# Values for three head pairs in five loads, keys and queries split and turned sooner, second-layer weight blocks loaded later: attention with a maxout layer on one core

## The chip, the cores and the metric

The kernel runs on one core of one Trainium2 chip. The metric is the device time of one launch in microseconds, as the median of a few runs. The core has TensorE (PE in the profile; its weight loads are PEld), VectorE (DVE), ScalarE (ACT), GpSimd (POOL) and SyncE (SP), which run side by side and wait for each other by semaphores. Transfers are issued by an engine's instruction queue, here nearly all by SP, and carried out by 16 DMA engines.

## The reference

```python
# q, k, v: (8, 12, 448, 64) float32; w1, w2, w3, w_out: (768, 768) float64; x is (3584, 768)
q_n, k_n = (rmsnorm(q, g_q), rmsnorm(k, g_k))
scores = scale * np.matmul(q_n, k_n.transpose(0, 1, 3, 2))
scores = scores - np.max(scores, axis=-1, keepdims=True)
attn = np.exp(scores)
attn = attn / (np.sum(attn, axis=-1, keepdims=True) + 1e-09)
attn_out = np.matmul(attn, v)
x = attn_out.transpose(0, 2, 1, 3).reshape(B * S, H * D)
h = np.maximum(np.maximum(x @ w1, x @ w2), x @ w3)
out = h @ w_out
```

Eight batches of 12 heads go through normalised attention; the heads of a batch side by side are the 448 rows of x that go through the maxout layer.

## The kernel before

**Work and pairs.** Two heads make a pair; there are 48 pairs (`g` = 0 to 47), six to a batch. A pair's 448 x 448 scores are made in four chunks `c` (three of 128 queries for each head, the last of 64 for both). The first six pairs (`PLAIN`) use float32 matmuls and let TensorE turn keys, queries and weights. From pair 6 on, each float32 operand is split into an upper and a lower float16 part, and the turning is done by transposing transfers: `turn_rows` (keys and queries), `turn_weights` (softmax weights, tiles `pp` to `pt`).

**Beats.** `beat(g, i)` writes out the program in order, 12 beats to a pair. No scheduler moves anything afterwards: what is written first on an engine or on a queue goes first there. `later(n, work)` puts work n beats on. Between its score matmuls TensorE gets matmuls of the maxout layer (`thirds`, from `ffn`); that filling exists from pair 6 on, when the first batch's x is done.

**Keys and queries of a pair** (from pair 6 on). `scale_rows` (GpSimd) makes `kn` and `qn` in beats 8 and 9 two pairs ahead. `upper_rows` (ScalarE) casts to float16, `lower_rows` (GpSimd) subtracts, `turn_rows` issues a transposing transfer on SP, and `swap_keys` issues two copies `kt<-kt` on SP that bring each head's keys to the other half of the partitions. Before, these stand in beats 0 and 1, 2 and 3, 4 and 5, and 7 of the pair before. The first scores of a pair are written in beat 11; their second matmul reads what the two copies bring.

**Values.** `load_v(g)` loads one pair's values in four transfers into a tile `vr` (7 buffers). Each row of 64 values is 256 bytes; rows 0 to 63 of one head and 384 to 447 of the other fill the last quarter. Three beats later `largest_v` (VectorE) takes the largest absolute value per row; `bound_v(b)` joins those of a batch and spreads the bound by a matmul (`most<-v_most`). In pair 0 the values of pairs 0 to 6 are loaded in beats 0 to 6, later one pair's in beat 6. `scale_v`, `upper_v` and `lower_v` split the values from pair 6 on; `add_values` multiplies them with `pt` (`av`).

**Weight blocks.** 24 blocks of float64 weights pass through two buffers `raw` of 768 KB: 18 of the first layer, one each 4 beats, then 6 of the second, one each 8 beats. `prep_block(n)` scales a block's upper words (ScalarE, L186), three steps on VectorE over the next beats put float32 together (L194, L198, L203), and 5 beats after it `load_raw` issues the load of block n+2 into the buffer that is then free. The instruction waits in SP's queue for the last VectorE step.

Of the kernel before, what the change touches and what calls it, by code (L numbers as in the profile page):

```python
# [9 lines left out]
F32 = mybir.dt.float32  # L10
# [6 lines left out]
P = 128  # L17
# [18 lines left out]
PLAIN = 6  # L36
# [6 lines left out]
def qknorm_attention_maxout_ffn_kernel(  # L43
# [35 lines left out]
    nc = tc.nc  # L79
    B, H, S, D = q.shape  # L80
    DM, DF = w1.shape
    DO = w_out.shape[1]
    NP = H // 2
    NQ = 4
    UNITS = 7
# [6 lines left out]
    G = B * NP  # L92
# [4 lines left out]
    sb = ctx.enter_context(tc.tile_pool(name="sb", bufs=2))  # L97
# [18 lines left out]
    def later(beats, work, last=False):  # L116

        due.setdefault(clock[0] + beats, ([], []))[last].append(work)
# [63 lines left out]
    def rebias(raw):  # L182


        upper = raw.bitcast(F32).rearrange("p (n t) -> p n t", t=2)[:, :, 1]
        nc.scalar.activation(upper, upper, AF.Copy, scale=REBIAS)  # L186
# [42 lines left out]
    def plain(t, n):  # L229
        return t[:, n + 1].rearrange("p a n -> p (a n)").bitcast(F32)  # L230

    def prep_block(n):
        kind, ft, j = blocks[n]
        raw = raws[n]
        f = plain(w_sb, n) if kind == "in" else plain(wo_sb, ft)
        rebias(raw)

        for stage in range(3):
            later(2 + stage, lambda stage=stage: decode(raw, f, stage), True)
        if kind == "out":  # L240
            later(5, lambda: row_largest(o_row[:, ft:ft + 1], f), True)
        later(5, load_raw)
        if j == NJ - 1:
            later(5, lambda: bound_in(ft), True)
        elif kind == "out" and ft == NFT - 1:
            later(6, bound_out)
# [76 lines left out]
    st = {}  # L323
# [20 lines left out]
        load_rows(g, "kr", k, first if g < LOADS else (nc.scalar,))  # L344


    def load_v(g):

        b, pr = divmod(g, NP)
        t = sb.tile([P, 2, 4, D], F32, name="vr", bufs=7)  # L350
        rows = v[b, 2 * pr:2 * pr + 2]
        for h in range(2):
            nc.sync.dma_start(
                out=t[:, h, 0:3], in_=rows[h, 0:3 * P].rearrange("(u p) d -> p u d", p=P)
            )
        for half, part in zip(HALVES, (rows[:, 3 * P:S], rows[:, 0:LEFT])):
            nc.sync.dma_start(out=t[half, :, 3], in_=part.rearrange("h p d -> p h d"))
        st.setdefault(g, {})["vr"] = t


    def squares(g, what):
        s = st[g]
        src = s[what + "r"]
        sq = sb.tile([P, UNITS, D], F32, name="sq", tag="rows", bufs=5)
        if g < 2:
            nc.scalar.activation(sq, src, AF.Square)  # L366
        else:
            nc.gpsimd.tensor_tensor(out=sq, in0=src, in1=src, op=ALU.mult)
        s["sq" + what] = sq
# [21 lines left out]
    def scale_rows(g, what):  # L391
        s = st[g]
        rows, ri = s.pop(what + "r"), s["ri"][:, KQ[what]]
        n = sb.tile([P, UNITS, D], F32, name=what + "n", tag="rows", bufs=5)
        s[what + "n"] = n
        on = nc.gpsimd if g else nc.vector
        on.tensor_tensor(
            out=n, in0=rows,
            in1=ri.rearrange("p (n o) -> p n o", o=1).broadcast_to([P, UNITS, D]),
            op=ALU.mult,  # L400
        )
        if what == "k":
            return
        s.pop("ri")
        if g >= PLAIN:
            nc.gpsimd.tensor_tensor(
                out=n, in0=n,
                in1=gain.rearrange("p (o d) -> p o d", o=1).broadcast_to([P, UNITS, D]),
                op=ALU.mult,
            )  # L410


    def upper_rows(g, what):
        s = st[g]
        n = s.pop(what + "n")
        parts = sb.tile([P, UNITS, 2, D], F16, name=what + "p", bufs=1)
        nc.scalar.copy(parts[:, :, 0], n)  # L417
        s[what + "p"] = parts, n

    def lower_rows(g, what):  # L420
        s = st[g]
        parts, n = s[what + "p"]
        nc.gpsimd.tensor_tensor(  # L423
            out=parts[:, :, 1], in0=n, in1=parts[:, :, 0], op=ALU.subtract
        )
        s[what + "p"] = parts

    def turn_rows(g, what):
        s = st[g]
        parts = s.pop(what + "p")  # L430
        if what == "k":
            t = sb.tile([P, 2, UNITS * P], F16, name="kt", bufs=2)
            to = t[:, 0].rearrange("p (n r) -> p n r", n=UNITS)
        else:
            t = sb.tile([P, 8, P], F16, name="qt", bufs=2)
            to = t[:, :UNITS]
        nc.sync.dma_start_transpose(out=to, in_=parts.rearrange("p n a d -> p (n a d)"))
        s[what + "s"] = t
# [44 lines left out]
    v_rows = {}  # L483
    v_down = const.tile([P, B], F32, name="v_down")
    v_up = const.tile([P, B], F32, name="v_up")

    def largest_v(g):
        b, pr = divmod(g, NP)
        if b not in v_rows:
            v_rows[b] = sb.tile([P, NP], F32, name="v_rows", bufs=2)  # L490
        row_largest(
            v_rows[b][:, pr:pr + 1], st[g]["vr"].rearrange("p h n d -> p (h n d)")
        )

    def bound_v(b):
# [21 lines left out]


    def scale_v(g):
        vr = st[g]["vr"].rearrange("p h n d -> p (h n d)")  # L520
        nc.gpsimd.tensor_scalar(
            out=vr, in0=vr, scalar1=v_up[:, g // NP:g // NP + 1], scalar2=1.0,
            op0=ALU.mult, op1=ALU.mult,
        )

    def upper_v(g):
        s = st[g]
        vp = sb.tile([P, 2, 8, D], F16, name="vp", bufs=2)
        nc.scalar.copy(vp[:, 0], s["vr"].rearrange("p h n d -> p (h n) d"))  # L529
        s["vp"] = vp  # L530

    def lower_v(g):
        s = st[g]
        vr, vp = s.pop("vr"), s["vp"]
        nc.gpsimd.tensor_tensor(  # L535
            out=vp[:, 1], in0=vr.rearrange("p h n d -> p (h n) d"), in1=vp[:, 0],
            op=ALU.subtract,
        )

# [76 lines left out]
    def pt_plain(s):  # L616
        return s["pt"].rearrange("p u s -> p (u s)").bitcast(F32).rearrange(
            "p (h u s) -> p h u s", h=2, u=4
        )
# [113 lines left out]
    def add_values(g):  # L733
        s = st[g]
        av = ps_a.tile([P, 512], F32, name="av", tag="a")
        s["av"] = av
        if g < PLAIN:
            vr, pt = s["vr"], pt_plain(s)
            for u in range(4):
                rows = HALVES[0] if u == 3 else slice(0, P)  # L740
                for h, half in enumerate(HALVES):
                    nc.tensor.matmul(
                        av[half, :S], vr[rows, h, u], pt[rows, h, u],
                        start=u == 0, stop=u == 3,
                    )
            return
        vp, vs, pt = s["vp"], s["vs"], s["pt"]
        steps = [(part, u, u) for u in range(4) for part in range(2)]
        steps += [(2, u, 4 + u) for u in range(3)]
        for n, (part, u, block) in enumerate(steps):  # L750
            for h, half in enumerate(HALVES):
                values = vs[:, h, u] if part == 2 else vp[:, part, 4 * h + u]
                nc.tensor.matmul(  # L753
                    av[half, :S], values, pt[:, 7 * h + block, SHIFT[h]:SHIFT[h] + S],
                    start=n == 0, stop=n == len(steps) - 1,
                )
# [150 lines left out]
    for i, src in enumerate((g_q, g_k)):  # L907
        nc.scalar.dma_start(
            out=gains[:, i], in_=src.rearrange("(o d) -> o d", o=1).broadcast_to([P, D])
# [75 lines left out]
    def beat(g, i):  # L985
        w, n = g - 1, g + 2
        c, part = divmod(i, 3)
        k = 4 * g + c
# [41 lines left out]
        if g + 1 < G:  # L1030
            if g + 1 < PLAIN:
                if i in (1, 4):
                    turn_whole(g + 1, "kq"[i // 4])
                if i in (2, 5):
                    keep_whole(g + 1, "kq"[i // 5])
            else:
                if i in (0, 1):
                    upper_rows(g + 1, "kq"[i])
                if i in (2, 3):
                    lower_rows(g + 1, "kq"[i - 2])  # L1040
                if i in (4, 5):
                    turn_rows(g + 1, "kq"[i - 4])
                if i == 7:
                    swap_keys(g + 1)

        if n < G:
            if i in (0, 3):
                squares(n, "kq"[i // 3])
            if i in (2, 5):
                sum_squares(n, "kq"[i // 3])  # L1050
            if i in (5, 7):
                inv_rms(n, "kq"[i // 7])
            if i in (8, 9):
                scale_rows(n, "kq"[i - 8])

        if g == 0 and i < 7:
            load_v(i)
            later(3, lambda: largest_v(i))
        if 0 < g < G - 6 and i == 6:
            load_v(g + 6)  # L1060
            later(3, lambda: largest_v(g + 6))
        if g == 0 and i == 9:
            bound_v(0)
        if g > 1 and g % NP == 0 and g < G and i == 1:
# [66 lines left out]
```

## Time and profile before

| what | value |
|---|---|
| median of 3 runs | 1071.95 us (1071.87 to 1072.58) |
| the profiled execution | 1070.58 us, of which span 1068.8 us |
| PE busy | 992.4 us, 93% of the span |
| DVE, ACT, POOL busy | 705.5, 637.9, 615.2 us |
| mean granted TensorE clock | 0.974 |
| transfers of one pair's values | 2 of 96 KB and 2 of 32 KB, 192 in all |

In the views, L753 is line 753 of the kernel, `out<-in` names what an instruction writes and reads, `x12` is a count. A row of the waits reads: engine, output and line that waited, what it waited for, total us, times, longest. A row of the timeline reads: start, duration, engine, line, operation, and in brackets the idle time of the engine before it with what ended it. "SPq" is SP's queue. A row of the windows gives busy time and instruction count of PE, PEld, DVE, ACT and POOL, then the granted clock, the mean busy share of the DMA engines and GB/s.

### The profile page before, as it was taken

What the parts mean: (1) busy time and instruction counts of PE and PEld (TensorE: products, weight loads), DVE (VectorE), ACT (ScalarE), POOL (GpSimd) and SP (SyncE); (2) the same over time, 40 slices, a digit from 0 to 9 for tenths busy, and PEclk for the clock granted to TensorE, in tenths of its full rate; (3) what the DMA queues carried; (4) which work ended last, traced back from release to release, by engine and by line L of the source; (5) the groups of instructions that cost most, each with busy time, mean ns of one, the idle gap of its engine ahead of it and who ended that gap; (6) DMA issues with size and microseconds to landing.
All of it is one profiled execution on the core that took longest, in us unless ns stands there. A gap on an engine that the chain in (4) does not pass through costs nothing. (4 is left out here: it accounts for less than half of the span.)

```text
span 1068.8 us, 17394 instructions
## 1 busy us (share of the span) xinstructions
PE 992.4 (93%) x5850; PEld 527.0 (49%) x5850; DVE 705.5 (66%) x1348; ACT 637.9 (60%) x1437; POOL 615.2 (58%) x661
## 2 busy tenths in 40 slices
PE   5598869899889999999999999999999999999998
PEld 3354434444445555455544555545544555555555
DVE  3789978888757776677666766777577756761110
ACT  3478868657746566565755666657566675652101
POOL 5257878856746767467666675766657666510000
PEclk9699979989989999999999999999999999999999
DMA  5655659896999999999999999999989999672001
GB/s 144 162 146 161 162 154 202 175 178 123 195 180 158 162 177 206 157 183 161 198 164 173 164 189 191 168 169 174 184 169 176 164 194 182 115 121 76 1 1 59
DMA packets 526681, 166.20 MB, mean 156 GB/s; under 512 B 502912, under 2 KB 522368, under 8 KB 526592
## 3 DMA queue, kind: packets, MB, share of 16 engines
q1 hardware_dynamic: 463584, 149.10, 71.7%
q10 hardware_dynamic: 63008, 16.00, 8.3%
q8 instruction: 46, 0.75, 0.3%
q14 instruction: 43, 0.35, 0.1%
HBM read 53.54 MB, written 11.01 MB: 60 GB/s over the span
## 5 line engine op out<-in xcount | busy, mean ns | idle before, releaser
L782 PE MATMUL acc<-xt,w_sb 128*128 128x448 f16 x2592 | 515.4, 354 | 0.0
L782 PEld LDWEIGHTS <-w_sb 128*128 128x128 f16 x2592 | 252.1, 98 | 244.2 <-issue 15.3
L611 ACT ACTIVATE sc<-sc,nm 128x448 f32<-128x448 f32 x294 | 178.8, 608 | 163.7 <-DVE nm L595 159.2
L595 DVE TENSOR_REDUCE nm<-sc 128x2 f32<-128x896 f32 x192 | 186.2, 970 | 95.1 <-PE sc L580 58.2
L697 ACT ACTIVATE pp<-sc,rs 128x448 f16<-128x448 f32 x294 | 172.8, 633 | 119.4 <-issue 65.8
L707 DVE SCALAR_TENSOR_TENSOR pp<-sc,rs,pp 128x448 f16<-128x448 f32 x294 | 187.9, 674 | 3.1 <-ACT pp L697 3.1
L573 PE MATMUL sc<-kt,qt 128*128 128x448 f16 x504 | 121.1, 358 | 34.4 <-DMA kt<-kt 22.5
L389 POOL TENSOR_TENSOR ri<-ri,half_neg 128x7 f32<-128x7 f32 x96 | 147.3, 1535 | 8.0
L842 PE MATMUL acc<-wo_sb,ht 128*128 128x384 f16 x864 | 148.3, 326 | 0.3 <-DVE ht L806 0.3
L811 POOL COPY hx<-ht 128x128 f16<-128x128 f16 x48 | 15.5, 323 | 204.4 <-DVE ht L806 204.4
L842 PEld LDWEIGHTS <-ht 128*128 128x128 f16 x864 | 83.3, 98 | 60.5 <-issue 4.7
L535 POOL TENSOR_TENSOR vp<-vr,vp 128x512 f16<-128x512 f32 x42 | 50.0, 1189 | 76.9 <-ACT vp L529 76.9
L573 PEld LDWEIGHTS <-qt 128*128 128x128 f16 x504 | 47.7, 98 | 86.2 <-DMA kt<-kt 29.1
L423 POOL TENSOR_TENSOR kp<-kn,kp 128x448 f16<-128x448 f32 x42 | 44.9, 1069 | 46.9 <-ACT kp L417 46.8
L753 PE MATMUL av<-pt,vp 128*64 128x448 f16 x672 | 71.6, 356 | 0.0
L375 DVE TENSOR_REDUCE ss<-sq 128x7 f32<-128x448 f32 x96 | 57.8, 603 | 12.5 <-ACT sq L366 9.0
L690 DVE TENSOR_SCALAR rs<-sc 128x2 f32<-128x2 f32 (+1 forms) x168 | 26.2, 156 | 52.7 <-ACT sc L611 52.7
L768 DVE SCALAR_TENSOR_TENSOR xt<-av,xt 128x448 f16<-128x448 f32 x42 | 26.2, 623 | 49.1 <-ACT xt L767 49.1
L423 POOL TENSOR_TENSOR qp<-qn,qp 128x448 f16<-128x448 f32 x42 | 43.4, 1034 | 23.0 <-ACT qp L417 23.0
L168 DVE TENSOR_REDUCE v_rows<-vr 128x1 f32<-128x512 f32 x48 | 32.8, 683 | 33.7 <-DMA vr<-in_v_dram 32.8
L796 DVE TENSOR_TENSOR m<-acc,m 128x448 f32<-128x448 f32 x48 | 29.6, 617 | 36.0 <-PE acc L782 35.3
L753 PEld LDWEIGHTS <-vp 128*64 128x64 f16 x672 | 34.5, 109 | 34.1 <-issue 12.2
(126 smaller groups left out, 1224.4 us busy)
## 6 DMA issues: line engine op xcount, KB each, us to landing
raw<-in_moe_w_dram SPq DMA_DIRECT2D x18, 768.0 KB, 4.5
kt<-kt SPq DMA_DIRECT2D x84, 112.0 KB, 2.3
vr<-in_v_dram SPq DMA_DIRECT2D x96, 96.0 KB, 2.8
out_dram<-osb SPq DMA_DIRECT2D x24, 384.0 KB, 3.5
kr<-in_k_dram ACTq DMA_DIRECT2D x34, 224.0 KB, 3.5
qr<-in_q_dram ACTq DMA_DIRECT2D x34, 224.0 KB, 4.6
raw<-in_moe_w_out_dram SPq DMA_DIRECT2D x6, 768.0 KB, 5.2
vs<-vp SPq DMA_DIRECT2D x84, 48.0 KB, 3.4
```

The source lines that it names most:

```text
L375: nc.vector.tensor_reduce(sums[g % 2][:, KQ[what]], sq, axis=AX, op=ALU.add)
L389: nc.gpsimd.tensor_tensor(out=ri, in0=ri, in1=half_neg[:, at], op=ALU.pow)
L423: nc.gpsimd.tensor_tensor(out=parts[:, :, 1], in0=n, in1=parts[:, :, 0], op=ALU.subtract)
L535: nc.gpsimd.tensor_tensor(out=vp[:, 1], in0=vr.rearrange("p h n d -> p (h n) d"), in1=vp[:, 0], op=ALU.subtract,)
L573: nc.tensor.matmul(sc[:, h, :S], qt[:, 4 * h + c], kt[:, n, keys[h]], start=n == 0, stop=n == 1,)
L595: nc.vector.tensor_reduce(nm[:, :n], sc[:, :n, :S], axis=AX, op=ALU.max, negate=True)
L611: nc.scalar.activation(to, sc[:, h, :S], AF.Exp, bias=nm[:, h:h + 1], accum_out=total,)
L697: nc.scalar.activation(pp[:, h, 0], sc[:, h, :S], AF.Copy, scale=rs[:, h:h + 1])
L707: nc.vector.scalar_tensor_tensor(out=pp[:, h, 1], in0=sc[:, h, :S], scalar=rs[:, h:h + 1], in1=pp[:, h, 0], op0=ALU.mult, op1=ALU.subtract,)
L753: nc.tensor.matmul(av[half, :S], values, pt[:, 7 * h + block, SHIFT[h]:SHIFT[h] + S], start=n == 0, stop=n == len(steps) - 1,)
L782: nc.tensor.matmul(acc[:, :S], wt[:, wp, c], xs[c][:, xp], start=(c == 0 and n == 0), stop=(c == NCT - 1 and n == 2),)
L842: nc.tensor.matmul(acc[:, :HW], lhs, wo_sb[:, f, wp, half * HW:(half + 1) * HW], start=(f == 0 and n == 0), stop=(f == NFT - 1 and n == 2),)
```

## The change

Values are loaded for three pairs at once: a tile holds six heads, in three transfers of 128 partitions x 6 heads x 64 and two of 64 x 6 x 64, with 3 buffers (of three times the size) instead of 7. Tiles 0 and 1 are loaded in beats 0 and 3 of pair 0, tile 2 in its beat 9, and from there one tile in beat 9 of every third pair. The largest value is taken once per tile, 5 or 8 beats after the load. Keys are cast in beat 11 of the pair before the one they were cast in, queries in beat 0 (each one beat sooner); the subtraction, the turning and the copies come two beats sooner (beats 0 and 1, 2 and 3, 5). Blocks loaded from within the second layer's steps are issued 9 beats instead of 5 after the step. The tag `rows` (squares and scaled rows) has 4 buffers instead of 5.

```diff
-        later(5, load_raw)
+        later(5 if kind == "in" else 9, load_raw)
...
-        t = sb.tile([P, 2, 4, D], F32, name="vr", bufs=7)
-        rows = v[b, 2 * pr:2 * pr + 2]
-        for h in range(2):
+        vr = sb.tile([P, NP, 4, D], F32, name="vr", bufs=3)
+        rows = v[b, NP * n:NP * (n + 1)]
+        for u in range(3):
             nc.sync.dma_start(
-                out=t[:, h, 0:3], in_=rows[h, 0:3 * P].rearrange("(u p) d -> p u d", p=P)
+                out=vr[:, :, u],
+                in_=rows[:, u * P:(u + 1) * P].rearrange("h p d -> p h d"),
             )
         for half, part in zip(HALVES, (rows[:, 3 * P:S], rows[:, 0:LEFT])):
-            nc.sync.dma_start(out=t[half, :, 3], in_=part.rearrange("h p d -> p h d"))
+            nc.sync.dma_start(out=vr[half, :, 3], in_=part.rearrange("h p d -> p h d"))
...
+    def values_of(g):
+        return v_tiles[g // 3][:, 2 * (g % 3):2 * (g % 3) + 2]
...
-        sq = sb.tile([P, UNITS, D], F32, name="sq", tag="rows", bufs=5)
+        sq = sb.tile([P, UNITS, D], F32, name="sq", tag="rows", bufs=4)
...
             else:
+                if i == 0:
+                    upper_rows(g + 1, "q")
                 if i in (0, 1):
-                    upper_rows(g + 1, "kq"[i])
+                    lower_rows(g + 1, "kq"[i])
                 if i in (2, 3):
-                    lower_rows(g + 1, "kq"[i - 2])
-                if i in (4, 5):
-                    turn_rows(g + 1, "kq"[i - 4])
-                if i == 7:
+                    turn_rows(g + 1, "kq"[i - 2])
+                if i == 5:
                     swap_keys(g + 1)
 
+        if PLAIN <= n < G and i == 11:
+            upper_rows(n, "k")
...
-        if g == 0 and i < 7:
-            load_v(i)
-            later(3, lambda: largest_v(i))
-        if 0 < g < G - 6 and i == 6:
-            load_v(g + 6)
-            later(3, lambda: largest_v(g + 6))
+        if g == 0 and i in (0, 3):
+            load_v(i // 3)
+            later(5, lambda: largest_v(i // 3))
+        if g % 3 == 0 and g + 6 < G and i == 9:
+            load_v(g // 3 + 2)
+            later(8, lambda: largest_v(g // 3 + 2))
```

On SP's queue in pair 0, before: the values of seven pairs, and then the third and fourth weight block (the number after a name tells buffers apart; line numbers differ between the two programs).

```order
L334 DMA qr_197<-in_q_dram 128x64
L353 DMA vr_215<-in_v_dram 128x3x64 x2
L357 DMA vr_215<-in_v_dram 64x2x64 x2
L333 DMA kr_220<-in_k_dram 128x3x64 x2
L334 DMA kr_220<-in_k_dram 128x64
...
L353 DMA vr_304<-in_v_dram 128x3x64 x2
L357 DMA vr_304<-in_v_dram 64x2x64 x2
L353 DMA vr_330<-in_v_dram 128x3x64 x2
L357 DMA vr_330<-in_v_dram 64x2x64 x2
L221 DMA raw_335<-in_moe_w3_dram 128x6x256
L221 DMA raw_377<-in_moe_w1_dram 128x6x256
```

The same place after:

```order
L334 DMA qr_197<-in_q_dram 128x64
L355 DMA vr_215<-in_v_dram 128x6x64 x3
L360 DMA vr_215<-in_v_dram 64x6x64 x2
L333 DMA kr_221<-in_k_dram 128x3x64 x2
L334 DMA kr_221<-in_k_dram 128x64
L333 DMA qr_232<-in_q_dram 128x3x64 x2
L334 DMA qr_232<-in_q_dram 128x64
L355 DMA vr_263<-in_v_dram 128x6x64 x3
L360 DMA vr_263<-in_v_dram 64x6x64 x2
L221 DMA raw_310<-in_moe_w3_dram 128x6x256
L355 DMA vr_342<-in_v_dram 128x6x64 x3
L360 DMA vr_342<-in_v_dram 64x6x64 x2
```

Ten value loads now stand ahead of the third block where 28 stood, and a third tile's five stand between the third and the fourth.

On SP's queue in a pair in the middle, before, from one pair's key transpose to the copies of its values:

```order
L437 DMA_TRANSPOSE kt<-kp 128x7x128
L437 DMA_TRANSPOSE qt<-qp 128x7x128
L720 DMA_TRANSPOSE pt<-pp 128x14x128
L353 DMA vr<-in_v_dram 128x3x64 x2
L357 DMA vr<-in_v_dram 64x2x64 x2
L444 DMA kt<-kt 64x896 x2
L720 DMA_TRANSPOSE pt<-pp 128x14x128 x2
L726 DMA_TRANSPOSE pt<-pp 128x7x64 x2
L546 DMA vs<-vp 64x2x192
L547 DMA vs<-vp 64x2x192
```

The same after, in a pair with a value load:

```order
L443 DMA_TRANSPOSE kt<-kp 128x7x128
L732 DMA_TRANSPOSE pt<-pp 128x7x64 x2
L443 DMA_TRANSPOSE qt<-qp 128x7x128
L552 DMA vs<-vp 64x2x192
L553 DMA vs<-vp 64x2x192
L450 DMA kt<-kt 64x896 x2
L726 DMA_TRANSPOSE pt<-pp 128x14x128
L824 DMA out_dram<-osb 128x768
L726 DMA_TRANSPOSE pt<-pp 128x14x128
L355 DMA vr<-in_v_dram 128x6x64 x3
L360 DMA vr<-in_v_dram 64x6x64 x2
L726 DMA_TRANSPOSE pt<-pp 128x14x128
```

The key copies stand ahead of the first weight transpose and no value load is in front of them; the key transpose stands ahead of the last chunk's two weight transposes, and the query transpose between these and the copies of the values.

On GpSimd around a pair's end, before:

```order
L521 TENSOR_SCALAR vr<-vr,v_up 128x512
L368 TENSOR_TENSOR sq<-kr 128x448
L535 TENSOR_TENSOR vp<-vr,vp 128x512
L423 TENSOR_TENSOR kp<-kn,kp 128x7x64
L423 TENSOR_TENSOR qp<-qn,qp 128x7x64
L368 TENSOR_TENSOR sq<-qr 128x448
```

And after:

```order
L527 TENSOR_SCALAR vr<-vr,v_up 128x512
L429 TENSOR_TENSOR kp<-kn,kp 128x7x64
L374 TENSOR_TENSOR sq<-kr 128x448
L541 TENSOR_TENSOR vp<-vr,vp 128x512
L429 TENSOR_TENSOR qp<-qn,qp 128x7x64
L374 TENSOR_TENSOR sq<-qr 128x448
```

The lower part of the keys now stands two places up, ahead of the squares and of the values' lower part. TensorE's own order is the same in both programs.

More of the change, by code (lines that the diff above doesn't have):

```diff
@@ L344, in load_k, with load_v @@
         load_rows(g, "kr", k, first if g < LOADS else (nc.scalar,))
-    def load_v(g):
-        b, pr = divmod(g, NP)
-        t = sb.tile([P, 2, 4, D], F32, name="vr", bufs=7)
-        rows = v[b, 2 * pr:2 * pr + 2]
-        for h in range(2):
+    v_tiles = {}
+    def load_v(t):
+        b, n = divmod(t, 2)
+        vr = sb.tile([P, NP, 4, D], F32, name="vr", bufs=3)
+        rows = v[b, NP * n:NP * (n + 1)]
+        for u in range(3):
             nc.sync.dma_start(
-                out=t[:, h, 0:3], in_=rows[h, 0:3 * P].rearrange("(u p) d -> p u d", p=P)
+                out=vr[:, :, u],
+                in_=rows[:, u * P:(u + 1) * P].rearrange("h p d -> p h d"),
             )
         for half, part in zip(HALVES, (rows[:, 3 * P:S], rows[:, 0:LEFT])):
-            nc.sync.dma_start(out=t[half, :, 3], in_=part.rearrange("h p d -> p h d"))
-        st.setdefault(g, {})["vr"] = t
+            nc.sync.dma_start(out=vr[half, :, 3], in_=part.rearrange("h p d -> p h d"))
+        v_tiles[t] = vr
+    def values_of(g):
+        return v_tiles[g // 3][:, 2 * (g % 3):2 * (g % 3) + 2]
     def squares(g, what):
@@ L393, in scale_rows @@
         rows, ri = s.pop(what + "r"), s["ri"][:, KQ[what]]
-        n = sb.tile([P, UNITS, D], F32, name=what + "n", tag="rows", bufs=5)
+        n = sb.tile([P, UNITS, D], F32, name=what + "n", tag="rows", bufs=4)
         s[what + "n"] = n
@@ L485, in qknorm_attention_maxout_ffn_kernel, with largest_v @@
     v_up = const.tile([P, B], F32, name="v_up")
-    def largest_v(g):
-        b, pr = divmod(g, NP)
+    def largest_v(t):
+        b, n = divmod(t, 2)
         if b not in v_rows:
-            v_rows[b] = sb.tile([P, NP], F32, name="v_rows", bufs=2)
+            v_rows[b] = sb.tile([P, 2], F32, name="v_rows", bufs=2)
         row_largest(
-            v_rows[b][:, pr:pr + 1], st[g]["vr"].rearrange("p h n d -> p (h n d)")
+            v_rows[b][:, n:n + 1], v_tiles[t].rearrange("p h n d -> p (h n d)")
         )
@@ L519, in scale_v @@
     def scale_v(g):
-        vr = st[g]["vr"].rearrange("p h n d -> p (h n d)")
+        vr = values_of(g).rearrange("p h n d -> p (h n d)")
         nc.gpsimd.tensor_scalar(
@@ L528, in upper_v @@
         vp = sb.tile([P, 2, 8, D], F16, name="vp", bufs=2)
-        nc.scalar.copy(vp[:, 0], s["vr"].rearrange("p h n d -> p (h n) d"))
+        nc.scalar.copy(vp[:, 0], values_of(g).rearrange("p h n d -> p (h n) d"))
         s["vp"] = vp
@@ L533, in lower_v @@
         s = st[g]
-        vr, vp = s.pop("vr"), s["vp"]
+        vp = s["vp"]
         nc.gpsimd.tensor_tensor(
-            out=vp[:, 1], in0=vr.rearrange("p h n d -> p (h n) d"), in1=vp[:, 0],
+            out=vp[:, 1], in0=values_of(g).rearrange("p h n d -> p (h n) d"), in1=vp[:, 0],
             op=ALU.subtract,
@@ L737, in add_values @@
         if g < PLAIN:
-            vr, pt = s["vr"], pt_plain(s)
+            vr, pt = values_of(g), pt_plain(s)
             for u in range(4):
```

## The prediction

> **What bounds the kernel now.** I read the page first (span, busy shares, slices), then the windows, then TensorE's waits by stage, and last the queue of SP where those waits end.
>
> ```profile
> span 1068.8 us, 17394 instructions
> ...
> PE 992.4 (93%) x5850; PEld 527.0 (49%) x5850; DVE 705.5 (66%) x1348; ACT 637.9 (60%) x1437; POOL 615.2 (58%) x661
> ...
> PE   5598869899889999999999999999999999999998
> ```
>
> ```profile
> 15.00:50.00 35.00, 21.20 (x93) 12.77 (x94) 21.70 (x32) 17.26 (x41) 15.83 (x18) 0.76 0.62 150
> 50.00:135.00 85.00, 76.37 (x457) 43.91 (x458) 76.96 (x100) 68.88 (x144) 60.19 (x46) 0.94 0.56 154
> 135.00:150.00 15.00, 7.89 (x39) 5.16 (x37) 10.02 (x17) 9.28 (x18) 10.50 (x8) 0.77 0.65 178
> 150.00:300.00 150.00, 126.78 (x719) 64.25 (x718) 120.83 (x231) 103.21 (x222) 106.62 (x104) 0.94 0.86 172
> 300.00:900.00 600.00, 590.97 (x3564) 309.13 (x3563) 415.67 (x842) 380.90 (x888) 389.53 (x440) 1.00 0.97 176
> ```
>
> TensorE is the bound from 300 us on: 9 us idle in 600. What can be won lies mostly earlier: 13.8 us idle from 15 to 50, 8.6 from 50 to 135 (there VectorE, 76.96 of 85 us busy, paces the float32 pairs), 7.1 from 135 to 150, 23.2 from 150 to 300. TensorE's order is the same after the change, so the span moves by what its idle time moves. Its waits in all, in 135 to 300, and in 300 to 900:
>
> ```profile
> PE sc L573 <- DMA kt<-kt: 22.5, 13, 6.1
> ...
> PE most L504 <- DVE v_most L497: 8.9, 2, 6.9
> ...
> PE sc L573 <- DMA kt<-kt: 15.0, 4, 6.1
> ...
> PE sc L573 <- DMA kt<-kt: 7.5, 9, 1.8
> ```
>
> The largest waits end on two things that the change touches: the key copies `kt<-kt` (22.5 us), and the bound on the values (one wait of 6.9 us).
>
> **The values at the start.** SP's queue, VectorE's waits from 15 to 50, VectorE's and ScalarE's work there:
>
> ```profile
> 22.65 0.96 SPq L353 DMA_DIRECT2D vr<-in_v_dram  x2
> 23.66 1.25 SPq L357 DMA_DIRECT2D vr<-in_v_dram  x2
> ...
> 37.55 1.26 SPq L357 DMA_DIRECT2D vr<-in_v_dram  x2
> 38.92 3.67 SPq L221 DMA_DIRECT2D raw<-in_moe_w_dram  x2
> ...
> DVE v_rows L168 <- DMA vr<-in_v_dram: 7.3, 6, 2.0
> ...
> 39.54 0.15 DVE L497 TENSOR_REDUCE v_most<-v_rows 128x1 f32<-128x6 f32 x1
> ...
> 51.07 0.55 DVE L194 TENSOR_SCALAR w_sb<-raw 128x768 uint32<-128x768 uint32 x1
> ...
> 43.51 0.88 ACT L186 ACTIVATE raw<-raw 128x768 f32<-128x768 f32 x1 [5.43 <-DMA raw<-in_moe_w_dram]
> ...
> 47.09 0.91 ACT L186 ACTIVATE raw<-raw 128x768 f32<-128x768 f32 x1
> ```
>
> SP issues from 22.65 to 38.81 almost without a break: six pairs' values at 2.2 us each, and one pair's queries. VectorE follows at that pace, `v_most` comes at 39.54, and the third weight block leaves at 38.92, so ScalarE waits 5.4 us for it. The prices:
>
> ```profile
> L353 SPq DMA_DIRECT2D vr<-in_v_dram x96: 367/496/1477, 15.9 to 846.5; - x96
> ...
> L357 SPq DMA_DIRECT2D vr<-in_v_dram x96: 600/630/1190, 17.1 to 847.7; - x96
> ...
> L336 SPq DMA_DIRECT2D kr<-in_k_dram x8: 386/644/1042, 81.9 to 236.8; - x8
> ...
> L168 DVE TENSOR_REDUCE v_rows<-vr x48: 666/686/687, 23.5 to 850.4; 128x1 f32<-128x512 f32 x48
> L168 DVE TENSOR_REDUCE most<-w_sb x6: 2534/2540/2543, 48.6 to 154.5; 128x1 f32<-128x2304 f32 x6
> L168 DVE TENSOR_REDUCE o_row<-wo_sb x6: 933/941/944, 164.5 to 237.2; 128x1 f32<-128x768 f32 x6
> ```
>
> No load of 128x6x64 exists. Its issue is bounded by 0.50 us (128x3x64, L353) below and 1.04 us (the longest of 128x7x64, L336) above; the half-partition ones by 0.63 and 1.19. A tile costs 2.8 to 5.5 us of SP; I take 2.8 at the start, where L353 and L357 run near their medians. Between 22.65 and the third block then stand the queries (16.2 - 6 x 2.2 = 3 us with what lies between) and one tile: SP is free at 28.5 instead of 38.9. The block must also wait for VectorE to be done with the first block. VectorE loses 7.3 us of waits, and two reductions of 1536 elements (941 + 768 x (2540 - 941)/1536 = 1741 ns, 3.5 us) replace six (4.1 us): `v_most` comes some 6.5 to 7.9 us sooner. The fourth block now stands behind a third tile of the same 768 KB; the third alone gains up to 10 us, but the fourth sets VectorE's step at 51.07. I take 6.5 us for the whole start, with ends 0 (the blocks arrive no sooner) and 10.4 (SP's lead in full). It is kept, since VectorE paces what follows and has no other long wait there.
>
> **The first float16 pair.** Here the copies leave 0.5 us behind a weight block:
>
> ```profile
> 137.29 0.38 SPq L221 DMA_DIRECT2D raw<-in_moe_w_dram  x1
> 137.77 1.17 SPq L444 DMA_DIRECT2D kt<-kt  x2
> ...
> 144.58 1.30 PE L573 MATMUL sc<-kt,qt 128*128 128x448 f16 x3 [6.15 <-DMA kt<-kt]
> ...
> 141.55 0.68 DVE L768 SCALAR_TENSOR_TENSOR xt<-av,v_up,xt 128x448 f16<-128x448 f32 x1
> 145.92 1.09 DVE L595 TENSOR_REDUCE nm<-sc 128x2 f32<-128x896 f32 x1 [3.69 <-PE sc L573]
> ...
> DMA to landing us min/median/max: 2.2/2.3/6.5
> ```
>
> They land 6.5 us after issue (the last row, their landings) where 2.3 is usual. Two beats sooner they leave ahead of that block, and the values' four loads (2.2 us) are no longer before them. TensorE's 6.15 us go; VectorE has work until 142.23, so the maximum at 145.92 can come 3.7 us sooner, or 4.4 without the reduction that stood before it. I take 4.0, ends 0 and 6.15. Next late are VectorE's own steps.
>
> **The other key copies.** 15.0 - 6.15 = 8.9 us until 300 and 7.5 later. The copies move two beats (a pair takes 18.9 us, SP's rows below from 340.33 to 359.26; 2 x 18.9/12 = 3.2 us) and lose 2.2 us of value loads in front. With 5.4 us the waits up to 1.8 us after 300 go whole, if their transposes keep up: I take 6.5 of 7.5, ends 3 and 7.5. Of the 8.9 I take 5, since VectorE is busy 120.83 of 150 us there and would be next late; ends 2 and 8.9.
>
> **What the sooner steps push back.** In a pair in the middle:
>
> ```profile
> 340.33 2.56 SPq L726 DMA_TRANSPOSE pt<-pp  x2
> ...
> 349.59 1.71 PE L753 MATMUL av<-pt,vp 128*64 128x448 f16 x16
> ...
> DMA to landing us min/median/max: 2.5/4.5/7.0
> ...
> 359.26 2.51 SPq L726 DMA_TRANSPOSE pt<-pp  x2
> ...
> 357.53 1.16 POOL L535 TENSOR_TENSOR vp<-vr,vp 128x512 f16<-128x512 f32 x1 [1.93 <-ACT vp L529]
> 360.57 1.04 POOL L423 TENSOR_TENSOR kp<-kn,kp 128x448 f16<-128x448 f32 x1 [1.88 <-ACT kp L417]
> ```
>
> The last chunk's second transpose starts at about 341.6, lands 4.5 us later (L726's median) at 346.1, and `av` starts at 349.59: 3.5 us of slack. Ahead of it now stands the key transpose, 1.3 us (half of the 2.56 for two), if GpSimd has `kp` ready. GpSimd's first step of that place started at 357.53, when ScalarE's cast let it; `kp` takes that place, is done at 358.6, and the last chunk's transposes left at 359.26: they go about 0.7 us later. ScalarE's casts move by a beat into its idle time (380.90 busy of 600). So this part costs nothing while the slack covers it, 1.3 us a pair if it were gone. Of the 14 tiles after the first two, 12 load in float16 pairs, in one burst of 768 KB where 256 KB went per pair. A copy behind such a block came 4.2 us late (6.5 against 2.3); the last chunk's transposes follow the burst by five beats, 7.9 us. I take 1.5 us for all bursts, ends 0 and 12 x (4.2 + 1.3 - 3.5) = 24. One reduction of 1.74 us instead of three of 0.69 may hold a maximum back by 1.05 us, 14 times; VectorE is idle 184 us of the 600. I take 0.5, ends 0 and 15.
>
> [...]
>
> Second-layer blocks 4 beats later: zero. The load leaves 9 beats after its predecessor's step, 7 of the 8-beat steps before its own, 11 us. The 4-buffer `rows` tag: zero, four tiles a pair come round once, and each is read within the pair.
>
> **The sum.** 6.5 + 4.0 + 5.0 + 6.5 - 1.5 - 0.5 = 20.0 us off the profiled execution's 1068.8 us span: 1048.8, and with the 1.8 us around it (1070.6 - 1068.8) 1050.6. The median of the runs is 1.4 us above that execution: 1052.0.
>
> **Rivals.** One: a load's issue grows with its rows, so that five loads cost SP what twelve did (6.6 us a tile). The start gains nothing, as the fourth block then leaves behind three tiles, and the rest stays: 1052 + 6.5 = 1058.5. Against it are L336 and L353. Chance 0.10.
>
> Two: VectorE becomes the bound wherever the copies no longer are, up to 300 us: the terms 4.0 and 5.0 go, 1061. For it speaks 120.83 of 150 us, against it that 3.69 us of VectorE's own idling end on these scores. Chance 0.09.
>
> Three: the bursts. The transposes behind them come late for `av`, by half the bound 12 us: 1052 + 10.5 = 1062.5, chance 0.08; by the whole, 24 us: 1074.5, chance 0.05. The DMA share of 0.97 speaks for it, the 7.9 us against it. [...]
>
> Four, slower: the key transpose stands at the head of SP's queue waiting for GpSimd, with the last chunk's transposes behind it. With a wait of x each of 41 pairs loses x + 1.3 - 3.5; the 22 us gained are gone at x = 2.7. With x = 2.9 it is 1072 - 22 + 29 = 1079. Against it: 358.6 lies ahead of 359.26. Chance 0.06.
>
> **How the numbers follow.** The forecast has 0.57 (alone 1045 to 1057), more than its terms, to 1041, has 0.05. The range 1043 to 1063 leaves out the whole burst, rival four and most of the better case, 0.15. Faster by over 0.2% (2.1 us, about what a measurement tells from no change): 0.57 + 0.05 + 0.10 + 0.09 + 0.08 = 0.89. Of the 0.11 left, rival four and part of the full burst are slower, 0.07, and 0.04 is the same.
>
> **What would show it.** The start: `v_most` near 33 us, the wait of `most` for it below 2 us, the third block's ScalarE step near 34. The copies: waits of `sc` for `kt<-kt` below 3 us in all. VectorE's waits for `vr` nearly gone. Wrong it would be with `av` waiting for `pt<-pp`, with SP waiting for GpSimd at the key transposes over 2 us a pair, or with TensorE's idle time from 150 to 300 still near 23 us.

## The result, and the profile after

The changed kernel takes 1047.97 us (median of 4 runs, 1045.91 to 1050.08), the kernel before 1072.12 us beside it (4 runs, 1071.87 to 1072.58): a ratio of 0.9774 [0.9754, 0.9795], 2.3% faster. The profiled execution took 1048.51 us, 1.9 us more than its span. The first lines of its page, and its windows:

```profile
span 1046.6 us, 17125 instructions
...
PE 987.6 (94%) x5850; PEld 524.4 (50%) x5850; DVE 709.9 (68%) x1316; ACT 638.1 (61%) x1437; POOL 617.6 (59%) x661
```

```profile
15.00:50.00 35.00, 29.34 (x166) 17.04 (x167) 30.57 (x38) 22.61 (x53) 22.06 (x23) 0.95 0.79 174
50.00:135.00 85.00, 70.47 (x420) 41.00 (x418) 82.12 (x102) 71.36 (x149) 65.03 (x47) 0.94 0.61 165
135.00:150.00 15.00, 11.65 (x45) 4.53 (x43) 12.15 (x21) 10.25 (x22) 11.62 (x11) 0.66 0.72 165
150.00:300.00 150.00, 132.45 (x751) 65.88 (x751) 120.93 (x224) 101.95 (x220) 106.93 (x106) 0.95 0.92 174
300.00:900.00 600.00, 596.82 (x3629) 315.67 (x3631) 419.61 (x838) 387.67 (x903) 394.11 (x448) 1.00 0.98 177
```

TensorE's idle time from 15 to 50 us fell from 13.8 to 5.7, from 150 to 300 from 23.2 to 17.6, from 300 to 900 from 9.0 to 3.2; from 50 to 135 it rose from 8.6 to 14.5, where VectorE is now busy 82 of 85 us. TensorE's waits, first in 135 to 300, then in 300 to 900:

```profile
PE sc L579 <- DVE pp L713: 8.4, 6, 2.7
PE av L759 <- DMA vs<-vp: 3.6, 1, 3.6
...
PE av L759 <- DMA vs<-vp: 2.2, 2, 1.2
PE av L759 <- DMA pt<-pp: 0.9, 1, 0.9
```

The 22.5 us of waits for key copies `kt<-kt` are gone. A new one is there: `av` waits for the copies of the values, `vs<-vp`. The start, on SP's queue, VectorE and ScalarE:

```profile
29.01 0.37 SPq L221 DMA_DIRECT2D raw<-in_moe_w_dram  x1
...
34.61 0.37 SPq L221 DMA_DIRECT2D raw<-in_moe_w_dram  x1
...
33.48 0.14 DVE L503 TENSOR_REDUCE v_most<-v_rows 128x1 f32<-128x2 f32 x1
33.59 0.96 DVE L203 SCALAR_TENSOR_TENSOR w_sb<-raw,w_sb 128x768 uint32<-128x768 uint32 x1
...
42.10 0.55 DVE L194 TENSOR_SCALAR w_sb<-raw 128x768 uint32<-128x768 uint32 x1
...
33.59 0.95 ACT L186 ACTIVATE raw<-raw 128x768 f32<-128x768 f32 x1 [2.08 <-DMA raw<-in_moe_w_dram]
```

`v_most` comes at 33.48 instead of 39.54, the third block's ScalarE step at 33.59 instead of 43.51, VectorE's first step on the fourth at 42.10 instead of 51.07.

**Where the gain comes from.** TensorE runs the same 5850 matmuls in the same order in all these kernels, so the start of one and the same matmul can be compared. Number 300 (80.6 us before) starts 10.9 us sooner, number 1400 (314.0 us before) 13.0 us, number 5800 22.4 us. In the table that is 10.9, 2.1 and 9.4 us for the three stretches, beside the same differences for every experiment (one profiled execution each; ratios of medians against the kernel before, with 95% intervals). A single execution is a rough measure: seven kernels of the table that run the same instructions up to number 300 lie between 9.6 and 11.5 us there, and a profiled execution can be 4 us from the median of its kernel (1039.43 beside 1043.52 us for `vs` sooner alone). A difference of 2 us between two rows of a column is therefore not read as an effect.

| kernel | median us | ratio | to no. 300 | 300 to 1400 | 1400 to 5800 |
|---|---|---|---|---|---|
| the change | 1047.97 | 0.9774 [0.9754, 0.9795] | 10.9 | 2.1 | 9.4 |
| values only | 1047.32 | 0.9784 [0.9760, 0.9807] | 11.5 | 3.1 | 11.0 |
| keys and queries only | 1086.74 | 1.0142 [1.0119, 1.0165] | 0.3 | 8.0 | -24.3 |
| second-layer blocks only | 1067.93 | 0.9967 [0.9952, 0.9982] | 0.8 | 3.3 | 1.2 |
| the change, twelve loads a tile | 1081.21 | 1.0095 [1.0071, 1.0120] | 5.1 | -2.0 | -13.2 |
| keys only, reduction later | 1050.92 | 0.9813 [0.9793, 0.9833] | 0.4 | 9.9 | 7.3 |
| values and blocks | 1045.12 | 0.9760 [0.9743, 0.9777] | 10.8 | 3.7 | 11.2 |
| the change, `vs` sooner, one block back | 1042.40 | 0.9732 [0.9712, 0.9753] | 11.4 | 10.3 | 9.6 |
| the change, blocks back | 1043.04 | 0.9747 [0.9723, 0.9770] | 9.6 | 5.1 | 9.9 |
| `vs` sooner, less VectorE work | 1041.66 | 0.9733 [0.9715, 0.9752] | 10.8 | 10.1 | 9.6 |
| before, reduction later | 1064.30 | 0.9942 [0.9926, 0.9958] | 2.8 | -0.8 | 6.8 |
| the change, `vs` sooner alone | 1043.52 | 0.9751 [0.9732, 0.9770] | 11.1 | 9.9 | 10.5 |
| `vs` sooner, third tile later | 1041.16 | 0.9729 [0.9710, 0.9748] | 11.6 | 6.1 | 9.1 |

### The profile page after: what moved, and what is told of

The parts are those of the page before. It is cut to its first block, busy times and chain, and to the rows that moved or that the text cites. A ratio compares the mean times of both kernels' runs of the same rounds, so it can differ in the third digit from the quotient of the medians.

```text
span 1046.6 us, 17125 instructions
## 1 busy us (share of the span) xinstructions
PE 987.6 (94%) x5850; PEld 524.4 (50%) x5850; DVE 709.9 (68%) x1316; ACT 638.1 (61%) x1437; POOL 617.6 (59%) x661
## 4 chain that ended last, share of the span: by engine, by line
PE 57%; DMA 1%; DVE 1%; ACT 0%; POOL 0%; issue 0%; SPq 0%
PE acc L788 33%; PE acc L848 12%; PE av L759 6%; PE sc L579 6%; PE sc L586 1%; DMA pt<-pp 0%; DVE nm L601 0%; ACT sc L617 0%; DMA vs<-vp 0%; POOL ri L395 0%; DVE ss L381 0%; DVE pp L713 0%; POOL kn L403 0%; SPq L552 0%; ACT osb L857 0%
## 5 line engine op out<-in xcount | busy, mean ns | idle before, releaser
L788 PE MATMUL acc<-xt,w_sb 128*128 128x448 f16 x2592 | 517.4, 355 | 0.0
L788 PEld LDWEIGHTS <-w_sb 128*128 128x128 f16 x2592 | 252.6, 98 | 245.7 <-issue 17.4
L579 PE MATMUL sc<-kt,qt 128*128 128x448 f16 x504 | 116.9, 355 | 12.7 <-DVE pp L713 8.4
L579 PEld LDWEIGHTS <-qt 128*128 128x128 f16 x504 | 48.7, 98 | 60.3 <-DVE pp L713 9.4
L808 ACT ACTIVATE ht<-acc 128x448 f16<-128x448 f32 x48 | 26.2, 547 | 41.7 <-DVE acc L802 41.7
```

What stands on the lines that cost most here:

```text
L579: nc.tensor.matmul(sc[:, h, :S], qt[:, 4 * h + c], kt[:, n, keys[h]], start=n == 0, stop=n == 1,)
L788: nc.tensor.matmul(acc[:, :S], wt[:, wp, c], xs[c][:, xp], start=(c == 0 and n == 0), stop=(c == NCT - 1 and n == 2),)
```

## The experiments

**The parts by themselves.** The new value tiles alone, which is the changed kernel with the keys and blocks put back:

```diff
-        later(5 if kind == "in" else 9, load_raw)
+        later(5, load_raw)
...
-                if i == 0:
-                    upper_rows(g + 1, "q")
                 if i in (0, 1):
-                    lower_rows(g + 1, "kq"[i])
+                    upper_rows(g + 1, "kq"[i])
                 if i in (2, 3):
-                    turn_rows(g + 1, "kq"[i - 2])
-                if i == 5:
+                    lower_rows(g + 1, "kq"[i - 2])
+                if i in (4, 5):
+                    turn_rows(g + 1, "kq"[i - 4])
+                if i == 7:
                     swap_keys(g + 1)
-        if PLAIN <= n < G and i == 11:
-            upper_rows(n, "k")
```

> Only the values' part (tiles of three pairs, five loads each); keys, queries and weight blocks stand as before. Theory (SP's issue of 28 loads paced the start, and the value loads in front of the key copies made part of the later waits): the start keeps its 10 to 11 us, the waits for kt<-kt fall from 22.5 to 8 us or less, time 1053 us (1050 to 1056). Rival (the key copies' waits are a matter of their beats alone): the start's 10 us and nothing else, kt<-kt near 20 us, 1061 us.

Measured 1047.32 us: the rival's and the theory's times were both too slow. The values alone are worth as much as the whole change. The key copies' waits fell from 22.5 to 8.4 us, with none after 300 us, and from 300 to 900 us the windows show TensorE idle for 0.5 us, though the key copies stand where they stood:

```profile
PE sc L579 <- DMA kt<-kt: 8.4, 3, 4.7
...
300.00:900.00 600.00, 599.50 (x3644) 315.95 (x3641) 422.37 (x841) 389.63 (x907) 398.37 (x450) 1.00 0.97 178
```

The key and query steps alone, in the kernel before: the lines of the change on `upper_rows`, `lower_rows`, `turn_rows` and `swap_keys`, as the change has them.

```diff
-                if i == 7:
+                if i == 5:
                     swap_keys(g + 1)
+        if PLAIN <= n < G and i == 11:
+            upper_rows(n, "k")
```

> Only the keys' and queries' steps sooner; values loaded pair by pair as before. Theory: the start stays as before (v_most near 39.5 us), the waits for kt<-kt after 300 us all go (9.5 us with what the wait rows do not count), those before 300 mostly pass on to VectorE: 1060 us (1057 to 1063). Rival (value loads in front still hold the copies back): half of that, 1066 us.

Measured 1086.74 us, 1.4% slower than before: both expectations wrong, even in sign. The second-layer blocks alone, `later(5 if kind == "in" else 9, load_raw)` in the kernel before:

> Only the second-layer blocks' loads 4 beats later. Theory: no change within 0.2%, 1072 us, since a later load waits less at SP's head but nobody waited for SP there. Rival: SP freed from waiting at 150 to 300 us gives 3 us or more, 1069 us or less; or the block, which now is issued in other beats, holds up the copies: 1074 us or more.

Measured 1067.93 us, 0.33% faster [0.18%, 0.48%]: the rival. The key copies' waits fell from 22.5 to

```profile
PE sc L573 <- DMA kt<-kt: 18.3, 13, 5.7
```

At 5 beats two of the four moved blocks left SP directly ahead of the key copies (0.6 us); at 9 beats one does.

**Is it the number of loads?** The changed kernel, each tile loaded by twelve transfers of the old shapes at the same beats, in place of the five:

```diff
+        for j in range(3):
+            two = rows[2 * j:2 * j + 2]
+            for h in range(2):
+                nc.sync.dma_start(
+                    out=vr[:, 2 * j + h, 0:3],
+                    in_=two[h, 0:3 * P].rearrange("(u p) d -> p u d", p=P),
+                )
+            for half, part in zip(HALVES, (two[:, 3 * P:S], two[:, 0:LEFT])):
+                nc.sync.dma_start(
+                    out=vr[half, 2 * j:2 * j + 2, 3], in_=part.rearrange("h p d -> p h d")
+                )
```

> The changed kernel with each tile of three pairs brought by twelve loads of the old shapes instead of five, at the same beats; the order of everything else is that of the changed kernel. Theory (the number of loads that SP issues is what cost the start): v_most comes 4 to 6 us later than 33.8 us, the fourth block some 8 us later, the start loses most of its 10 us, later little: 1056 us (1053 to 1060). Rival (beats and fewer reductions made the gain): 1050 us or less.

Measured 1081.21 us: slower than before, against both expectations. Its TensorE waits, and its burst on SP's queue (first and last row of six), and then the burst of five in the changed kernel:

```profile
PE av L763 <- DMA vs<-vp: 14.0, 12, 2.2
PE av L763 <- DMA pt<-pp: 13.8, 13, 3.7
...
349.62 1.23 SPq L357 DMA_DIRECT2D vr<-in_v_dram  x2
...
355.94 1.26 SPq L362 DMA_DIRECT2D vr<-in_v_dram  x2
```

```profile
339.37 2.51 SPq L355 DMA_DIRECT2D vr<-in_v_dram  x3
341.92 1.63 SPq L360 DMA_DIRECT2D vr<-in_v_dram  x2
```

Twelve loads hold SP from 349.62 to 357.20, 7.6 us, five for 4.2 us (3.0 at the medians below). The weight transposes behind come late, and so `av`. At the start twelve loads give 5.1 us where five give 10.9: about half of the start's gain is the lower number of loads. The rest stays with twelve loads; whether it is their order, the later beats or the two reductions in place of six was not taken apart.

**Why the keys alone lose.** The waits of that kernel on VectorE and TensorE, and one round of it on SP, VectorE, ScalarE, GpSimd and SP again:

```profile
DVE v_rows L168 <- DMA vr<-in_v_dram: 82.5, 39, 4.4
...
PE sc L573 <- DVE pp L707: 38.3, 36, 3.1
```

```profile
503.39 1.69 SPq L353 DMA_DIRECT2D vr<-in_v_dram  x2
...
505.13 1.36 SPq L357 DMA_DIRECT2D vr<-in_v_dram  x2
...
508.19 0.69 DVE L168 TENSOR_REDUCE v_rows<-vr 128x1 f32<-128x512 f32 x1 [1.67 <-DMA vr<-in_v_dram]
...
509.76 0.64 ACT L697 ACTIVATE pp<-sc,rs 128x448 f16<-128x448 f32 x1 [3.71 <-DVE rs L694]
...
511.14 0.57 ACT L417 CAST kp<-kn 128x448 f16<-128x448 f32 x1
...
512.34 1.03 POOL L423 TENSOR_TENSOR kp<-kn,kp 128x448 f16<-128x448 f32 x1
...
513.40 1.22 SPq L437 DMA_TRANSPOSE kt<-kp  x1
```

VectorE stands at a reduction whose values SP loaded late; the softmax step queued behind it is late, ScalarE's normalisation waits 3.71 us for that, its cast of the next keys stands behind, GpSimd's `kp` behind the cast, and the key transpose leaves 0.03 us after `kp`, with SP's queue standing. The reduction was then put two beats later and nothing else changed:

```diff
-            later(3, lambda: largest_v(g + 6))
+            later(5, lambda: largest_v(g + 6))
```

> The key and query steps alone (1086.7 us), with one number changed: VectorE's reduction of a pair's values comes 5 beats after their load instead of 3. Theory: the 15 us were lost because VectorE stood up to 4.4 us at the head of its queue for values that SP loaded late (82.5 us in 39 waits), which delayed ScalarE, GpSimd's kp and with it the key transpose on SP, so that the next values were late again. Then VectorE's waits for vr fall below 20 us, the scores' waits for pp from 38.3 to about 12, and the time is 1054 to 1064 us. Rival: SP's queue is simply too full with the key transpose waiting at its head; then another wait takes the place and the time stays above 1080.

Measured 1050.92 us: 35.8 us less for one number, below the theory's range. VectorE's waits for values fell less than expected (45.0 us are left, below 20 was expected), the scores' waits for `pp` about as far:

```profile
PE sc L573 <- DVE pp L707: 15.2, 13, 3.1
...
DVE v_rows L168 <- DMA vr<-in_v_dram: 45.0, 29, 4.1
```

So the sum of a wait does not tell its price; what is queued behind it counts. The edit touches VectorE's order alone, and SP's waits for GpSimd at the transposes of keys and queries fell with it, in their largest row from 108.2 to 53.5 us: this fits a loop, in which late values make the key transpose late and that makes the next values late. The rival, with the time above 1080 us, falls. The same edit in the kernel before:

> The kernel before, with VectorE's reduction of a pair's values 5 beats after their load instead of 3, and nothing else. Theory: VectorE's 32.8 us of waits for values cost little here, since TensorE's largest wait is for the key copies, which keep their place: 1068 to 1072 us. Rival: the values' waits alone hold the kernel back, and the key steps were needed for nothing: 1055 us.

Measured 1064.30 us, 0.58% faster [0.42%, 0.74%], between the two. Of the 8.8 us that its profile gains, 6.8 come after number 1400; the key copies' waits stay at 19.7 us:

```profile
PE sc L573 <- DMA kt<-kt: 19.7, 8, 6.2
```

The new value tiles also bring the reduction later, 5 or 8 beats after the load. No run has the five loads with the reduction at its old place, so how the 11.0 us that the values alone gain after number 1400 divide between fewer issues and a later reduction stays open.

**The new wait.** In the changed kernel, at the pair boundary before the wait of 3.6 us, on SP:

```profile
188.27 0.58 SPq L226 DMA_DIRECT2D raw<-in_moe_w_out_dram  x1
188.99 1.22 SPq L443 DMA_TRANSPOSE qt<-qp  x1
190.25 0.66 SPq L552 DMA_DIRECT2D vs<-vp  x1
190.96 0.62 SPq L553 DMA_DIRECT2D vs<-vp  x1
```

A 768 KB block leaves 2 us ahead of the copies `vs<-vp`, which land at about 197.0 us, 6 us after their issue (their median is 2.1). Values and blocks without the keys, in which no `av` waits:

> The values' five loads and the second-layer blocks 9 beats after, without the key and query steps. Theory: the key steps add nothing once SP is free of the values' loads, and the block move is worth what it was alone (3.3 us): 1044 us. Rival: the key copies' three waits left without the key steps (8.4 us) are not touched by the blocks, and the blocks at other beats only meet other transfers: 1047 us, as with the values alone.

Measured 1045.12 us, nearer to the theory's 1044; its interval overlaps that of the values alone, so nothing is shown for the blocks here. Next, the `vs` copies issued ahead of the query transpose, one block (n = 20) back at 5 beats:

```diff
-        later(5 if kind == "in" else 9, load_raw)
+        later(5 if kind == "in" or n == 20 else 9, load_raw)
...
-        if PLAIN <= w and i == 3:
-            shift_values(w)
...
         if i == 2 and w >= PLAIN:
             turn_weights(w, 3)
+            shift_values(w)
```

> The changed kernel with the values' copies vs<-vp issued ahead of the query transpose instead of behind it, and with the one second-layer block that stood just ahead of that transpose back at 5 beats. Theory: the 5.8 us that av waits for vs go, with 0.16 us more for each, and nothing else comes late: 1042 us. Rival: the last chunk's copies or VectorE's maxima are late next by as much (waits for pp, rs and sc are 14.9 us before 300 us): 1047 us.

Measured 1042.40 us, as the theory said. The blocks back alone, and the `vs` copies alone:

> The changed kernel with the second-layer blocks back at 5 beats: values and keys alone. Theory: the blocks at 9 beats are worth what they were alone, 3.3 us: 1051 us. Rival: with the key steps in place the move only shifts a block to stand ahead of the query transpose and the vs copies (a wait of 3.6 us): 1045 us. By the prediction the move is worth zero: 1048 us.

> The changed kernel with the vs copies ahead of the query transpose, the second-layer blocks left at 9 beats. Theory: the wait of 3.6 us comes of the block that stands in front, so moving the copies by 1.3 us takes only that much away: 1046 us. Rival: the copies' own place is the cause, and the blocks' is not: 1042 us, as with both.

Measured 1043.04 us and 1043.52 us. Both are rivals' results, though the intervals of both overlap the change's; only the kernel with both edits lies clear of it. In the second the theory had the order wrong: put to beat 2, the copies also go ahead of the block, as its SP queue shows:

```profile
185.54 0.65 SPq L552 DMA_DIRECT2D vs<-vp  x1
186.24 0.61 SPq L553 DMA_DIRECT2D vs<-vp  x1
186.91 0.58 SPq L226 DMA_DIRECT2D raw<-in_moe_w_out_dram  x1
```

Either edit takes this block from in front of these copies, and either removes the wait of 3.6 us. A block in front does not always cost that much: with the blocks back another one leaves ahead of the `vs` copies of the pair before, they land at 173.33 us, 4.2 us after their issue, and `av` needs them at 173.47 and does not wait.

```profile
166.50 0.53 SPq L226 DMA_DIRECT2D raw<-in_moe_w_out_dram  x1
...
169.11 0.63 SPq L553 DMA_DIRECT2D vs<-vp  x1
...
173.47 0.76 PE L759 MATMUL av<-pt,vs 128*64 128x448 f16 x6
```

**What the wait cost.** From matmul 700 to 900 the changed kernel takes 43.45 us, the one with sooner `vs` copies 37.22 (one execution each): 6.2 us for a wait of 3.6. The windows from 193 to 203 us, of the changed kernel and of the one with sooner copies (the number behind POOL's is the granted clock):

```profile
193.00:197.00 4.00, 0.54 (x6) 0.11 (x2) 2.70 (x6) 2.50 (x6) 3.83 (x5) 0.92 1.07 137
197.00:203.00 6.00, 5.88 (x21) 2.48 (x22) 2.57 (x6) 2.58 (x6) 2.25 (x3) 0.50 1.13 270
```

```profile
197.00:203.00 6.00, 6.00 (x34) 2.98 (x32) 5.28 (x8) 3.92 (x11) 4.13 (x4) 1.00 1.19 222
```

After the gap the granted clock is 0.50 for 6 us: 21 matmuls where 34 run at 1.00 (last row), so some 6 x (1 - 21/34) = 2.3 us more.

**Is VectorE the next bound up to 300 us?** In the kernel with sooner copies, the six reductions `o_row` over 96 of 768 columns, `row_largest(o_row[:, ft:ft + 1], f[:, 0:96])`:

> The kernel with the sooner vs copies (1042.4 us), with the six reductions of the output blocks' rows taken over 96 of their 768 columns: this leaves out seven eighths of that maximum, and some 5 of VectorE's 5.6 us for them, all between 150 and 300 us. Theory: what the copies lost there VectorE took over (it is busy 122 of 150 us, and the scores wait 11.5 us for pp): 3 to 5 us less, 1038 us. Rival: VectorE's own work there is off the path, and the waits for pp come of the order of the steps: 1042 us.

Measured 1041.66 us beside 1042.40 for the kernel it was made from: no difference that the intervals could show, so the theory's 3 to 5 us are not there. In the two profiles, from 135 to 300, TensorE's waits are 18.4 us in all instead of 23.1, but stretches at a lower granted clock (0.72 and 0.69 from 250 to 254 and from 280 to 284 us, where the kernel it was made from has 1.00 in both) took back 7.0 us instead of 2.4 (matmuls that start over 300 ns apart, less the usual 189 ns each). Whether VectorE bounds that stretch stays open.

**The third tile of values.** Loaded one pair later, in the same kernel:

```diff
-        if g % 3 == 0 and g + 6 < G and i == 9:
+        if (g == 1 or 0 < g < G - 6 and g % 3 == 0) and i == 9:
```

> The kernel with the sooner vs copies, with the third tile of values loaded one pair later, so that it no longer stands between the third and the fourth weight block. Theory: VectorE paces from the third block on and has no gap that the fourth block would fill, so the start stays as it is: 1042 us. Rival, by the prediction's start term: the fourth block behind the third tile takes about 4 of the 10.4 us away, and comes back: 1038 us.

Measured 1041.16 us, and 11.6 us won at matmul 300: the theory. The third and fourth block now follow each other on SP, and still

```profile
28.59 5.97 SPq L221 DMA_DIRECT2D raw<-in_moe_w_dram  x2
...
34.66 1.03 SPq L333 DMA_DIRECT2D kr<-in_k_dram  x2
...
33.17 0.96 DVE L203 SCALAR_TENSOR_TENSOR w_sb<-raw,w_sb 128x768 uint32<-128x768 uint32 x1
```

the queue stands with the fourth, whose issue of 0.37 us ends at 34.56: the block waits for its buffer, which VectorE gives free with the last step on the block in it, here at 33.17 + 0.96 = 34.13. In the changed kernel that step ends at 33.59 + 0.96 = 34.55 and the block leaves at 34.61, so the tile in front held nothing up. This is the fastest kernel of the study by its median, its interval overlapping that of the two before it.

## Why the prediction was right, point by point

The forecast was 1052.0 us, its range 1043 to 1063, faster with 0.89; 1047.97 us lies inside, 4.0 us below the forecast. That the sum is near is in part luck: errors of both signs met, and the term for the copies after 300 us had the wrong cause.

- **The start: 6.5 us predicted, 10.9 measured**, just above the upper end of 10.4. The three signs came: `v_most` at 33.48, the wait for it 1.8 us, ScalarE's step at 33.59. The step that failed is the fourth block that "now stands behind a third tile": the block waits until VectorE frees its buffer, with or without the tile. VectorE's first step on it came 9.0 us sooner, so little of the lead was lost.
- **The price of a load: right, and rival one is refuted.** The issues in the changed kernel, minimum, median and maximum in ns, are near those of the old shapes (367/496/1477 and 600/630/1190), with twice and three times the rows:

```profile
L355 SPq DMA_DIRECT2D vr<-in_v_dram x48: 368/573/1767, 13.8 to 789.7; - x48
...
L360 SPq DMA_DIRECT2D vr<-in_v_dram x32: 620/658/1401, 15.8 to 791.0; - x32
```

  The median issue hardly grew with the rows, 573 ns beside 496 for twice and 658 beside 630 for three times as many, so fewer loads were worth what the prediction took.
- **The first float16 pair and the copies until 300 us: 9.0 us predicted, 2.1 measured** in the changed kernel. The first pair gave 3.4 of its 4.0 (from matmul 500 to 600). The copies' own worth is near 9.0 in some kernels and not in others: the same stretch gives 9.9 to 10.3 us in four (keys with later reduction; `vs` sooner with one block back, with less VectorE work, and alone), but 8.0 with the keys alone, 6.1 with the third tile later and 5.1 with the blocks back, so it is not shown. The step that failed is "second-layer blocks 4 beats later: zero". It asked only whether the block arrives in time for its own step, not what SP and the DMA engines carry behind it: in the changed kernel one block came to stand ahead of the query transpose and the `vs` copies, at a price of 6.2 us in the profile (by the ratios of the medians 0.23 to 0.42%, 2.5 to 4.5 us), and alone the move gains 0.33%. The cover that was named for the sooner steps was the last chunk's transposes; the `vs` copies, which the key and query transposes also push back, were not priced.
- **The copies after 300 us: 6.5 us, less 2.0 for bursts and reductions; 9.4 measured.** All waits for `kt<-kt` went. More than 7.5 us could be won because a printed wait is short of the loss (below). But the cause was not the one named: without the sooner key steps the same stretch gives 11.0 us, and the steps alone lose 24.3.
- **Bursts, 1.5 us:** `av` waits 0.9 us for `pt<-pp` in 300 to 900, so rival three did not come. With twelve loads in the burst it did: 13.8 us, and 14.0 for `vs`.
- **VectorE's reduction, 0.5 us lost:** wrong in sign, as far as the experiments tell. With one reduction of 1.74 us, 8 beats after the load, all of VectorE's 32.8 us of waits for values are gone; two beats later alone are worth 0.58% in the kernel before. The prediction counted 7.3 us of these waits, at the start, and passed over the rest because VectorE has idle time; in these runs such a wait was paid by what stood behind it in the queue, not by the engine's idle time.
- **Rival four:** its sign came, and its loss did not. SP waits for GpSimd at the transposes, above the 2 us a pair that the prediction called wrong. The row holds those of keys and of queries; of its 37 waits 29 are at key transposes, with 78.8 us in all, 2.7 us each:

```profile
SPq L443 <- POOL sq L374: 89.7, 37, 5.3
```

  By its own sum 2.7 + 1.3 - 3.5 leaves 0.5 us in each of the 29, 14.5 us, and `av` waits 0.9 us for `pt<-pp` in all. The kernel with the keys alone waits 3.0 us at each of 33 key transposes (100.2 us) and is slower, but by the loop through VectorE's queue: its `av` waits 0.3 us for `pt<-pp` and 2.9 for `vs<-vp`.
- **Rival two** stays unsettled, as above. The `rows` tag with 4 buffers was not tried by itself.

## What to carry to other kernels

When a load is moved, look first at which engine has the instruction that waits for it, and what stands behind that instruction: two beats for one reduction were worth 36 us in one order and 7 in another. A moved transfer has to be priced by what it stands in front of, and by how long those behind it can wait, and not only by whether it arrives in time: the copies `vs<-vp` landed 6 us after their issue behind one 768 KB block and 4.2 behind another, where their median is 2.1, and `av` waited 3.6 us for the first and not for the second. Parts of a change need not add up: here three parts worth +24, -15 and +3 us alone made 24 together. Fewer, larger loads paid by what SP saves (4.2 us a burst instead of 7.6), and probably by the later reductions too, which were not taken apart from them.

## What the runs showed of the hardware beyond what was expected

- TensorE's granted clock was lower behind two of three gaps. After 3.58 us without a matmul, in the changed kernel, the granted clock was 0.50 for 6 us. It was 0.63 in the four us behind a wait of 2.69 us (first row, changed kernel), and 1.00 behind one of 2.73 us (second row, with sooner `vs` copies), so in these runs the length of a single wait did not decide it:

```profile
284.00:288.00 4.00, 3.56 (x12) 1.55 (x13) 2.74 (x6) 2.64 (x6) 2.00 (x3) 0.63 1.04 204
```

```profile
252.00:256.00 4.00, 4.00 (x28) 2.17 (x29) 3.66 (x7) 3.49 (x10) 2.48 (x5) 1.00 0.88 172
```

  Between matmuls 560 and 1400 stretches at a lower granted clock cost some 8 us before, some 7 after and 2.4 with sooner `vs` copies and one block back, counted as above; with the `vs` copies sooner alone they cost some 4, so this too varies.
- Printed waits between float16 matmuls are too short. Such matmuls start 189 ns apart in an unbroken row (the median from number 1400 to 5800, before and after), but each is shown with some 352 ns (the median of L579 and L788, after), so every break costs about 352 - 189 ns = 0.16 us more than its row says, and breaks below that don't show. Between the score matmuls after number 1400 the starts lay 9.7 us beyond that cadence in 27 places before, where the waits list 7.5 us in 9; after the change it is 0.01 us.
